# Laying softmax reciprocals by block, and moving logit sums and row evictions between engines, in an attention and expert kernel

## The chip, the cores and the metric

The kernel runs on one core of a Trainium2 chip. The metric is the device time of one execution in microseconds (us). A core has TensorE (matrix products; PE in the profile, and PEld for its weight loads), VectorE (DVE), ScalarE (ACT), GpSimd (POOL) and SyncE (SP, which issues DMAs). Each engine runs its own instructions in the order in which the program gives them, and waits for the others on semaphores.

## The reference, cut to what matters

```
scores = q @ k^T / sqrt(64)                  # q, k, v: 8 batches, 8 heads, 576 rows, 64 columns
attn = exp(scores - max), zero where scores < max - tau
attn = attn / (sum(attn) + 1e-9)
x = (attn @ v) as 4608 rows of 512           # row = batch and position, 8 heads side by side
logits = x @ w_gate                          # 8 experts
each row gets one expert: (row, expert) pairs by falling logit, at most 576 rows for an expert
out[rows of e] = relu(x[rows of e] @ w1[e]) @ w2[e]
```

All is in float32.

## The kernel before, in words

There are two stages: attention (`attention`, the first 469 us of the span) and the experts (`Router`, `moe`). The change is in the first.

**Tiles and slots.** A batch has four pairs of heads. For each pair the 576 rows of both heads make nine tiles of 128 rows: tiles 0 to 7 hold 128 rows of one head each, tile 8 holds the last 64 rows of both heads, head 0 on partitions 0 to 63 and head 1 on 64 to 127. That last block is called the tail here. The loop over `s_` goes in slots of two tiles and is a software pipeline written out by hand: in slot `s_` TensorE computes the scores of tiles `2s+4` and `2s+5` (`score`, L69, into the PSUM tile `sc`, two buffers), VectorE scales them and takes the row maximum (`mx`, L74), GpSimd adds tau to get the threshold `nb` (L75), ScalarE takes the exponential (`ex`, L86), VectorE zeroes what lies under the threshold and sums the row into `den` (`stt`, L90) for the two tiles before, TensorE transposes the two tiles before those (`tr`, L98, into the one buffer `tb`), and ScalarE evicts what was transposed in the slot before (`trev`, L113 and L115). Transposes of the tail go through `left`, and ScalarE evicts them in `leftev` (L125 to L128).

**Product with v.** It is queued in `queue` with a slot for each piece and taken out by `columns`, after the scores of the slot. Columns 0 to 255 of a batch's 576 accumulate in the PSUM bank `xo0`, columns 256 to 575 in `xo1` (`pv_unit`, L152; `pl_unit`, L162 for the tail keys). ScalarE evicts each into `xt` (`evict`, L142). Within a slot L162, or a first piece of L152, can open `xo1` directly behind the scores.

**What a batch leaves.** After the last pair of batch b, `rd_calc` makes the reciprocals `rd` of `den` on VectorE, and `finish(b)` appends units to `aux`. `whole` takes one of them out at the end of a slot when bank `xo1` is free; TensorE fills the bank, the returned function goes to `later`, and `flush` runs it in the next slot, behind the scores and ahead of `trev`. The units are:
- `lg_unit` (two): products of `xt` with the gate weights, four heads' pairs at 32-partition offsets (L179), evicted by ScalarE (L184). The first also multiplies the tail's reciprocals by the constant matrix `swap` (L181), which exchanges the partition halves, and four VectorE copies of 64 partitions (L186, L187) put both heads' reciprocals on both halves, in `rm`.
- `lgt_unit`: transposes of the logits of blocks 0 to 3 (L191). VectorE multiplies them by the reciprocals in two instructions, one for each head of the pairs (L196), and sums over the eight heads (L197) into `Lg`.
- `lgm_unit`: the same for the tail (L201, L206, L207), on partitions 0 to 63 for even batches and 64 to 127 for odd ones.
- `xt_unit` (five, only for batches 0 and 1 here): transposes of `xt` into rows (L213). VectorE evicts the rows into `xr` (L221), GpSimd copies the eight reciprocals of each row beside them, and a DMA writes both to `xrows`. For the other batches these units run after the attention and ScalarE evicts them (L223).

For the last batch the logit units run straight through, in the two `sc` buffers (`bank_g`), and the router begins behind them. It reads `Lg` for batches 0 to 6 first (`prep(0,28)`), then the rest.

Of the kernel before, what the change touches and what calls it, by code (L numbers as in the profile page):

```python
# [9 lines left out]
F32 = mybir.dt.float32  # L10
# [3 lines left out]
AF = mybir.ActivationFunctionType  # L14
ALU = mybir.AluOpType
AX = mybir.AxisListType
# [3 lines left out]
PPB=8; LTB=1; VTB=4; HOLD=1; XW=520; NBO=2; NDEF=4; XTB=4; XTY=1.05; XT0=2.0; XRB=2  # L20


def attention(ctx, tc, qk, vl, tau, wgd, xrows, xts, Lg, nb_batches, ident, swap, R, after_first):
    nc=tc.nc
    V=nc.vector; A=nc.scalar; G=nc.gpsimd; T=nc.tensor
    NP=nb_batches*4; NT=NP*9
# [28 lines left out]
    SC={}; NBI={}; TH={}; PB={}; DEN={}  # L55
    def den_of(p):
        b=p//4
        if b not in DEN: DEN[b]=wk.tile([128,4,9],F32,name="den")
        return DEN[b]
    def score(t):  # L60

# [8 lines left out]
    ZB={}  # L70
# [16 lines left out]
    def stt(t):  # L87
        p,i=divmod(t,9)
        pv=pview(t)
        V.scalar_tensor_tensor(pv,ZB.pop(t).rearrange("p a b -> p (a b)"),NBI[t][:,1:2],pv,op0=ALU.is_le,op1=ALU.mult,accum_out=den_of(p)[:,p%4,i:i+1])  # L90

# [70 lines left out]
    def bank_g(b,sh):  # L164
        if b<nb_batches-1: return bank_v(sh,1)
        t=ps_s.tile([128,2,512],F32,name="sc")[:,0]
        return t.rearrange("p (a b) -> p a b",a=sh[1]) if len(sh)==3 else t

    RD={}
    def rd_calc(b):  # L170
        rd=wk.tile([128,4,9],F32,name="rd",bufs=XTB+NBO); RD[b]=rd
        V.tensor_scalar(rd,DEN[b],1e-9,None,op0=ALU.add)
        V.reciprocal(rd,rd)
    LT={}
    def lg_unit(b,f):
        if f==0: LT[b]=wk.tile([128,S+D],F32,name="lt",bufs=LTB)
        ps=bank_g(b,[128,512]); q=FQ[f]; n=q.stop-q.start; rd=RD[b]
        for j in range(4):
            T.matmul(ps[32*j:32*j+32,:n],wg[:,j],XT[b][:,j,q],start=True,stop=True,tile_position=(0,32*j))  # L179
        if f==0:  # L180
            T.matmul(ps[:,256:260],swap,rd[:,:,8],start=True,stop=True)  # L181
            rm=wk.tile([128,4,2],F32,name="rm",bufs=XTB+NBO); RD["m",b]=rm
        def ev():
            A.activation(LT[b][:,q],ps[:,:n],AF.Copy)  # L184
            if f==1: G.tensor_scalar(LT[b][:,S:],LT[b][:,S-D:S],1.0,0.0,op0=ALU.mult,op1=ALU.add); return
            V.tensor_copy(rm[0:64,:,0],rd[0:64,:,8]); V.tensor_copy(rm[64:128,:,1],rd[64:128,:,8])  # L186
            V.tensor_copy(rm[0:64,:,1],ps[0:64,256:260]); V.tensor_copy(rm[64:128,:,0],ps[64:128,256:260])  # L187
        return ev
    def lgt_unit(b):
        ps=bank_g(b,[128,4,128])  # L190
        for c in range(4): T.transpose(ps[:,c],LT[b][:,c*128:(c+1)*128],ident)  # L191
        def ev():
            w=wk.tile([128,4,2,4,8],F32,name="lw",bufs=1)
            lv=ps.rearrange("p c (j r) -> p c j r",j=4)
            for h in range(2):
                V.tensor_tensor(w[:,:,h],lv[:,:,:,8*h:8*h+8],RD[b][:,:,h:8:2].rearrange("p j c -> p c j").unsqueeze(3).to_broadcast([128,4,4,8]),op=ALU.mult)  # L196
            V.tensor_reduce(Lg[:,4*b:4*b+4,:],w.rearrange("p c h j e -> p c e (h j)"),axis=AX.X,op=ALU.add)  # L197
        return ev
    def lgm_unit(b):
        ps=bank_g(b,[128,4,128])  # L200
        T.transpose(ps[:,0],LT[b][:,512:640],ident)  # L201
        r=slice(64*(b%2),64*(b%2)+64)
        def ev():
            w=wk.tile([128,4,2,8],F32,name="lwm",bufs=1)
            lv=ps[:,0].rearrange("p (j r) -> p j r",j=4)[:,:,:16].rearrange("p j (h e) -> p j h e",h=2)
            V.tensor_tensor(w[r],lv[r],RD["m",b][r].unsqueeze(3).to_broadcast([64,4,2,8]),op=ALU.mult)  # L206
            V.tensor_reduce(Lg[r,32+b//2,:],w[r].rearrange("p j h e -> p e (j h)"),axis=AX.X,op=ALU.add)  # L207
        return ev
    def xt_unit(b,c,k=1):
        ps=bank_v([128,4,128],k)  # L210
        n=128 if c<4 else 64
        for j in range(4):
            T.transpose(ps[:n,j],XT[b][:,j,c*128:c*128+n],ident)  # L213
        early=b<nb_batches-NDEF-NBO
        if early: xr=wk.tile([128,XW],F32,name="xr",bufs=XRB)
        else: xr=wk.tile([128,2,S],F32,name="pp",bufs=PPB)[:,0,:XW]
        def ev():
            src=RD[b][:,:,2*c:2*c+2] if c<4 else RD["m",b][0:64]
            fv=xr[:n,512:XW].rearrange("p (j h) -> p j h",j=4); xv=xr[:n,:512].rearrange("p (j d) -> p j d",j=4)
            if early:  # L220
                V.tensor_copy(xv,ps[:n]); G.tensor_scalar(fv,src,1.0,0.0,op0=ALU.mult,op1=ALU.add)  # L221
            else:
                A.activation(xv,ps[:n],AF.Copy); A.activation(fv,src,AF.Copy)  # L223
            nc.sync.dma_start(xrows[b*S+c*128:b*S+c*128+n,:],xr[:n])
        return ev

# [1 line left out]

    queue=[]; aux=[]; later=[]; late=[]; late2=[]; st={"last":-9,"slot":0}
    def push_pair(p):
        b,j=divmod(p,4)
        def when(n): return lambda: have.get((p,n),1<<30)+HOLD<=st["slot"]
# [20 lines left out]
    def finish(b):  # L255
        aux.extend([(0,lambda: lg_unit(b,0)),(0,lambda: lg_unit(b,1)),(1,lambda: lgt_unit(b)),(0,lambda: lgm_unit(b))])
        rows=[lambda k=1,c=c: xt_unit(b,c,k) for c in range(5)]
        if nb_batches-NDEF-NBO<=b<nb_batches-NDEF:
            nc.sync.dma_start(xts[b],XT[b]); late2.extend(rows)
        elif b<nb_batches-NDEF: aux.extend([(0,x) for x in rows])  # L260
        else: late.extend(rows)
    def flush():
        for k,g in later: g(); k[0]=True
        later.clear()
    def columns(all=False):
        n=0
        while queue and queue[0][1]():
# [7 lines left out]
        return n  # L275
    def whole():
        if aux and free_v(1) and st["slot"]>=st["last"]+aux[0][0] :
            r=aux.pop(0)[1](); st["last"]=st["slot"]
            later.append((banks[1][-1],r))

    idle=cst.tile([128,128],BF16,name="idle"); V.memset(idle,0.0)
    load(0)
# [7 lines left out]
    for s_ in range(-2,NT//2+2):  # L290
        st["slot"]=s_
        sc_=[t for t in (2*s_+4,2*s_+5) if 0<=t<NT]; tr_=[t for t in (2*s_,2*s_+1) if 0<=t<NT]
        ev_=[t for t in (2*s_-2,2*s_-1) if 0<=t<NT]; tt_=[t for t in (2*s_+2,2*s_+3) if 0<=t<NT]
        p8=[(t//9,n) for n,x in enumerate((tr_,ev_)) for t in x if t%9==8]
        if sc_ and sc_[0]%9==8: sc_.reverse()
        for t in sc_: score(t)
        for p,n in p8: left(p,n,sc_[-1] if sc_ else None)

        flush()
        for t in ev_:  # L300
            p,i=divmod(t,9)
# [623 lines left out]
def build(tc, qk, vl, tau, wgd, cst_d, w1, w2, out, off, nb=8):  # L925
    nc=tc.nc
    with ExitStack() as ctx:
        ctx.enter_context(tc.manual_schedule())
        cp=ctx.enter_context(tc.tile_pool(name="cst",bufs=1))
        dr=ctx.enter_context(tc.tile_pool(name="dr",bufs=1,space=bass.MemoryType.DRAM))  # L930
        xrows=dr.tile([8*S,XW],F32,name="xrows")
        xts=dr.tile([8,128,4,S],F32,name="xts")
        ident=cp.tile([128,128],F32,name="ident"); make_identity(nc,ident)
        swap=cp.tile([128,128],F32,name="swap")
        nc.vector.tensor_copy(swap[:,0:64],ident[:,64:128]); nc.vector.tensor_copy(swap[:,64:128],ident[:,0:64])
        Lg=cp.tile([128,NC_,8],F32,name="Lg")
# [24 lines left out]
```

## Time and profile before

| | |
|---|---|
| median of 3 runs | 990.44 us (988.67 to 991.09) |
| the profiled execution | 993.25 us, of which the span 991.4 us |
| TensorE busy, whole span | 955.4 us (96%) |
| VectorE busy | 782.1 us (79%) |
| ScalarE busy | 635.1 us (64%) |
| GpSimd busy | 261.0 us (26%) |
| granted TensorE clock | 0.988 of full speed |

A row of instructions reads: line, engine, operation, what it writes and reads, shapes, count; behind the bars the busy time and the mean of one in ns, and the idle time in front of them with what ended it. A row of the timeline reads: start, duration, engine, line, operation, count, and in brackets the idle time in front. A row of the waits reads: who waited for whom, the sum in us, how often, the longest. A float32 matrix product shows as two records of the same instruction.

### The profile page before, as it was taken

To read this page: it belongs to the slowest core of one execution; us is meant where nothing else is said; L and a number is where in the kernel's file an instruction comes from. 1 tells how busy PE (TensorE), PEld (TensorE's weight loads), DVE (VectorE), ACT (ScalarE), POOL (GpSimd) and SP (SyncE) were. 2 spreads that over 40 slices of the span, in tenths; PEclk is the share of its full clock that TensorE was granted. 3 is DMA by queue.
4 is the path that set the end of the run, shared out by engine and by line. 5 is a ranking of instruction groups with operands and counts; after the bars stand their busy time and mean duration, and the time that the engine had idled before them with its cause. 6 is when DMAs were issued, how large, how long until landed. Compare 5 with 4: busy or idle time off the path is not lost.

```text
span 991.4 us, 24055 instructions
## 1 busy us (share of the span) xinstructions
PE 955.4 (96%) x9141; PEld 709.3 (72%) x9141; DVE 782.1 (79%) x2158; ACT 635.1 (64%) x1257; POOL 261.0 (26%) x411
## 2 busy tenths in 40 slices
PE   7999999999999999998779999999999999999996
PEld 4556665666566556665679688897988979898995
DVE  7999999999999999995679778687787786525220
ACT  6899989898998999996645344243452534545340
POOL 2333334333333333331020323221302213320202
PEclk9999999999999999999979999999999999999998
DMA  6233244234533233303760605343433435341101
GB/s 252 73 110 121 72 153 151 85 142 148 180 109 121 98 120 93 114 3 139 257 211 20 226 28 172 101 137 110 137 124 118 140 100 166 112 137 47 38 11 42
DMA packets 35858, 116.98 MB, mean 118 GB/s; under 512 B 4384, under 2 KB 5024, under 8 KB 35232
## 3 DMA queue, kind: packets, MB, share of 16 engines
q1 hardware_dynamic: 28352, 92.85, 27.5%
q0 software_dynamic: 5888, 19.03, 6.1%
q10 hardware_dynamic: 1504, 3.59, 1.2%
q8 instruction: 72, 1.18, 0.5%
q14 instruction: 42, 0.34, 0.1%
HBM read 93.01 MB, written 21.38 MB: 115 GB/s over the span
## 4 chain that ended last, share of the span: by engine, by line
PE 83%; DVE 8%; issue 3%; DMA 3%; ACT 2%; POOLq 0%; SPq 0%; DVEq 0%; ACTq 0%
PE pf L791 21%; PE pf L823 19%; PE sc L69 13%; PE xo L152 12%; PE tb L98 8%; DVE pp L90 2%; DVE z L74 2%; PE pt L736 2%; PE xo L162 2%; PE xo L213 1%; PE rps L444 1%; PE xo L179 1%; DMA out_dram<-y,idx 1%; PE sc L98 1%; DVE cmp L376 1%
## 5 line engine op out<-in xcount | busy, mean ns | idle before, releaser
L75 POOL TENSOR_SCALAR nb<-nb,taub 128x1 f32<-128x1 f32 x288 | 149.7, 520 | 286.6 <-DVE z L74 246.4
L86 ACT ACTIVATE pp<-z,nb 128x576 f32<-128x576 f32 x256 | 193.5, 773 | 44.3 <-DVE z L74 40.2
L74 DVE TENSOR_SCALAR_CACHE_REDUCE z<-sc 128x576 f32<-128x576 f32 x288 | 205.8, 750 | 10.7 <-PE sc L69 8.8
L90 DVE SCALAR_TENSOR_TENSOR pp<-z,nb,pp 128x576 f32<-128x576 f32 x256 | 199.8, 813 | 0.3
L823 PE MATMUL pf<-w2h,H 128*128 128x512 f32 x576 | 195.2, 402 | 0.7 <-DVE H L376 0.7
L69 PE MATMUL sc<-qk 64*128 64x288 f32 (+1 forms) x1280 | 181.3, 427 | 3.2 <-DVE z L74 1.3
L152 PE MATMUL xo<-pt,vt 128*64 128x320 f32 (+1 forms) x1024 | 156.3, 422 | 0.0
L113 ACT ACTIVATE pt<-tb 128x512 f32<-128x512 f32 x256 | 139.4, 590 | 2.5 <-PE tb L98 1.6
L823 PE MATMUL pf<-w2l,H 128*128 128x512 f32 x320 | 128.3, 401 | 0.0
L830 POOL DMA_INDIRECT out_dram<-y,idx x40 | 43.8, 1096 | 310.3 <-ACT y L826 242.1
L823 PEld LDWEIGHTS pf<-w2h,H 128*128 128x128 f32 x576 | 106.5, 189 | 20.2 <-DVE H L376 1.6
L98 PEld LDWEIGHTS tb<-ident,pp 64*128 64x128 f32 x2048 | 75.2, 139 | 60.1 <-issue 25.5
L69 PEld LDWEIGHTS sc<-qk 64*128 64x128 f32 (+1 forms) x1280 | 94.6, 180 | 31.8 <-DVE z L74 5.7
L791 PE MATMUL pf<-xh,w1h 128*128 128x288 f32 (+2 forms) x512 | 110.1, 301 | 0.7 <-ACT xh L737 0.7
L791 PE MATMUL pf<-xl,w1h 128*128 128x288 f32 (+2 forms) x512 | 110.1, 301 | 0.0
L791 PE MATMUL pf<-xh,w1l 128*128 128x288 f32 (+2 forms) x512 | 109.8, 300 | 0.0
L826 ACT ACTIVATE y<-pf 128x512 f32<-128x512 f32 x40 | 23.9, 598 | 129.0 <-PE pf L823 120.8
L152 PEld LDWEIGHTS xo<-pt,vt 128*64 128x64 f32 x1024 | 61.2, 136 | 59.3 <-issue 33.1
L98 PE MATMUL tb<-ident,pp 64*128 64x64 f32 x2048 | 94.0, 229 | 5.8 <-ACT pt L113 5.8
L803 ACT ACTIVATE hf<-pf 128x576 f32<-128x576 f32 x56 | 36.6, 653 | 90.8 <-PE pf L791 81.7
L791 PEld LDWEIGHTS pf<-xh,w1h 128*128 128x128 f32 x512 | 82.0, 190 | 1.5 <-ACT xh L737 1.1
L791 PEld LDWEIGHTS pf<-xh,w1l 128*128 128x128 f32 x512 | 82.0, 189 | 0.5 <-issue 0.4
(199 smaller groups left out, 1322.4 us busy)
## 6 DMA issues: line engine op xcount, KB each, us to landing
qk<-qk_dram SPq DMA_DIRECT2D x31, 864.0 KB, 4.7
vt<-vl_dram SPq DMA_DIRECT2D x32, 576.0 KB, 3.8
w2s<-w_dram SPq DMA_DIRECT2D x32, 512.0 KB, 5.1
w1s<-w_dram SPq DMA_DIRECT2D x28, 512.0 KB, 4.3
xrows<-pp SPq DMA_DIRECT2D x24, 260.0 KB, 2.2
xts<-xt SPq DMA_DIRECT2D x2, 1152.0 KB
pt<-xts SPq DMA_DIRECT2D x2, 1152.0 KB, 8.7
xrows<-xr SPq DMA_DIRECT2D x8, 260.0 KB, 2.2
```

What stands on the lines that cost most here:

```text
L69: T.matmul(sc[o,f,:HS], kd["q",h][r,c], kd["k",h][r,:],start=True,stop=True)
L74: V.tensor_scalar(z,SC.pop(t)[:,:,:HS],-0.125,None,op0=ALU.mult,op1=ALU.min,accum_out=nb[:,0:1])
L75: G.tensor_scalar(nb[:,1:2],nb[:,0:1],taub[:,0:1],None,op0=ALU.add)
L86: A.activation(pview(t),ZB[t].rearrange("p a b -> p (a b)"),AF.Exp,bias=NBI[t][:,0:1],scale=-1.0)
L90: V.scalar_tensor_tensor(pv,ZB.pop(t).rearrange("p a b -> p (a b)"),NBI[t][:,1:2],pv,op0=ALU.is_le,op1=ALU.mult,accum_out=den_of(p)[:,p%4, ...
L98: g=slice(64*r,64*r+64); T.transpose(o[:,r],x[r%len(x)][g],ident[g,g])
L113: A.activation(PT[p][:,i%2,:,(i//2)*128:(i//2+1)*128].rearrange("p k (r q) -> p r k q",r=2),tb,AF.Copy)
L152: T.matmul(xo[64*h:64*h+64,:q.stop-q.start],v[:,f,128*u+64*h:128*u+64*h+64],PT[p][:,h,u,q],start=new,stop=last,skip_group_check=True)
L791: T.matmul(ps[:,h,:n],s[w][:,k,f*128:(f+1)*128],s[x][:,k,cols[h]],start=(i==0),stop=(i==11))
L803: A.activation(hf,ps[:,:,:HS],AF.Relu)
L823: T.matmul(ps[:,0,:],H[:,f,c:c+128],s[w][:,f],start=(f==0 and j==0),stop=e)
L830: G.indirect_dma_start(out=out,out_offset=IOA(ap=s["idx"][:n,t:t+1],axis=0),in_=y[:n],in_offset=None)
```

## The change

- `den` and `rd` are laid by block of 128 rows, `[128, 5, 4, 2]`: block, pair of heads, head. In the tail's block, GpSimd sets all eight columns to one when the tile is made; `stt` writes head 0's column.
- The matrix `swap` and the tile `rm` go. `dup` holds two matrices: the product with `dup[:,h]` puts the tail's reciprocals of head h on both partition halves. Two products (in `twice`) write eight columns behind the logits in the bank, and one ScalarE copy puts them back into `rd`. The four VectorE copies go.
- `logits` serves blocks and tail alike: one VectorE product for both heads, and the sum over heads as three GpSimd additions, halving each time. The last batch keeps VectorE's reduction. `lw` (one buffer) is now shared by both uses.
- ScalarE evicts the rows of batches 0 and 1 as of the others. In these slots the eviction is put into `behind` and runs after the slot's `trev`, not ahead of it.

```diff
-        if b not in DEN: DEN[b]=wk.tile([128,4,9],F32,name="den")
+        if b not in DEN: DEN[b]=wk.tile([128,5,4,2],F32,name="den"); G.memset(DEN[b][:,4],1.0)
...
-accum_out=den_of(p)[:,p%4,i:i+1])
+accum_out=den_of(p)[:,i//2,p%4,i%2:i%2+1])
...
+    def lg_ev(b,f,ps):
+        q=FQ[f]; A.activation(LT[b][:,q],ps[:,:q.stop-q.start],AF.Copy)
+    def twice(b,ps):
+        for h in range(2):
+            T.matmul(ps[:,:,h],dup[:,h],RD[b][:,4,:,0],start=True,stop=True)
+    def lg_unit(b,f):
+        ps=bank_g(b,[128,512]); rd=RD[b]
+        lg_mm(b,f,ps)
+        if f==0: twice(b,ps[:,256:264].rearrange("p (j h) -> p j h",h=2))
         def ev():
-            A.activation(LT[b][:,q],ps[:,:n],AF.Copy)
+            lg_ev(b,f,ps)
             if f==1: G.tensor_scalar(LT[b][:,S:],LT[b][:,S-D:S],1.0,0.0,op0=ALU.mult,op1=ALU.add); return
-            V.tensor_copy(rm[0:64,:,0],rd[0:64,:,8]); V.tensor_copy(rm[64:128,:,1],rd[64:128,:,8])
-            V.tensor_copy(rm[0:64,:,1],ps[0:64,256:260]); V.tensor_copy(rm[64:128,:,0],ps[64:128,256:260])
+            A.activation(rd[:,4].rearrange("p j h -> p (j h)"),ps[:,256:264],AF.Copy)
...
+    def logits(b,c0,c1,ps,r,o):
+        n=c1-c0; w=wk.tile([128,4,4,2,8],F32,name="lw",bufs=1)[r,:n]; m=r.stop-r.start
+        lv=ps[r].rearrange("p c (j r) -> p (c j) r",r=32)[:,:,:16].rearrange("p m (h e) -> p m h e",h=2)
+        V.tensor_tensor(w.rearrange("p c j h e -> p (c j) h e"),lv,RD[b][r,c0:c1].rearrange("p c j h -> p (c j) h").unsqueeze(3).to_broadcast([m,4*n,2,8]),op=ALU.mult)
+        if b==nb_batches-1: V.tensor_reduce(Lg[r,o:o+n,:],w.rearrange("p c j h e -> p c e (j h)"),axis=AX.X,op=ALU.add); return
+        G.tensor_tensor(w[:,:,0:2],w[:,:,0:2],w[:,:,2:4],op=ALU.add); G.tensor_tensor(w[:,:,0],w[:,:,0],w[:,:,1],op=ALU.add)
+        G.tensor_tensor(Lg[r,o:o+n,:],w[:,:,0,0],w[:,:,0,1],op=ALU.add)
...
-            src=RD[b][:,:,2*c:2*c+2] if c<4 else RD["m",b][0:64]
+            src=RD[b][:n,c]
...
-            if early:
-                V.tensor_copy(xv,ps[:n]); G.tensor_scalar(fv,src,1.0,0.0,op0=ALU.mult,op1=ALU.add)
-            else:
-                A.activation(xv,ps[:n],AF.Copy); A.activation(fv,src,AF.Copy)
+            A.activation(xv,ps[:n],AF.Copy)
+            if early: G.tensor_scalar(fv,src,1.0,0.0,op0=ALU.mult,op1=ALU.add)
+            else: A.activation(fv,src,AF.Copy)
...
-        elif b<nb_batches-NDEF: aux.extend([(0,x) for x in rows])
+        elif b<nb_batches-NDEF: aux.extend([(0,x,behind) for x in rows])
...
             trev(t); have[p,f"t{i}"]=s_
+        flush(behind)
...
-        swap=cp.tile([128,128],F32,name="swap")
-        nc.vector.tensor_copy(swap[:,0:64],ident[:,64:128]); nc.vector.tensor_copy(swap[:,64:128],ident[:,0:64])
+        dup=cp.tile([128,2,128],F32,name="dup")
+        for h in range(2):
+            for a in range(2): nc.vector.tensor_copy(dup[:,h,64*a:64*a+64],ident[:,64*h:64*h+64])
```

More of the change, by code (lines that the diff above doesn't have):

```diff
@@ L20, with attention @@
 PPB=8; LTB=1; VTB=4; HOLD=1; XW=520; NBO=2; NDEF=4; XTB=4; XTY=1.05; XT0=2.0; XRB=2
-def attention(ctx, tc, qk, vl, tau, wgd, xrows, xts, Lg, nb_batches, ident, swap, R, after_first):
+def attention(ctx, tc, qk, vl, tau, wgd, xrows, xts, Lg, nb_batches, ident, dup, R, after_first):
     nc=tc.nc
@@ L89, in stt @@
         pv=pview(t)
-        V.scalar_tensor_tensor(pv,ZB.pop(t).rearrange("p a b -> p (a b)"),NBI[t][:,1:2],pv,op0=ALU.is_le,op1=ALU.mult,accum_out=den_of(p)[:,p%4,i:i+1])
+        V.scalar_tensor_tensor(pv,ZB.pop(t).rearrange("p a b -> p (a b)"),NBI[t][:,1:2],pv,op0=ALU.is_le,op1=ALU.mult,accum_out=den_of(p)[:,i//2,p%4,i%2:i%2+1])
     PT={}; PL={}; TB={}
@@ L170, in rd_calc @@
     def rd_calc(b):
-        rd=wk.tile([128,4,9],F32,name="rd",bufs=XTB+NBO); RD[b]=rd
+        rd=wk.tile([128,5,4,2],F32,name="rd",bufs=XTB+NBO); RD[b]=rd
         V.tensor_scalar(rd,DEN[b],1e-9,None,op0=ALU.add)
@@ L174, in attention, with lg_mm @@
     LT={}
-    def lg_unit(b,f):
+    def lg_mm(b,f,ps):
         if f==0: LT[b]=wk.tile([128,S+D],F32,name="lt",bufs=LTB)
-        ps=bank_g(b,[128,512]); q=FQ[f]; n=q.stop-q.start; rd=RD[b]
+        q=FQ[f]; n=q.stop-q.start
         for j in range(4):
             T.matmul(ps[32*j:32*j+32,:n],wg[:,j],XT[b][:,j,q],start=True,stop=True,tile_position=(0,32*j))
-        if f==0:
-            T.matmul(ps[:,256:260],swap,rd[:,:,8],start=True,stop=True)
-            rm=wk.tile([128,4,2],F32,name="rm",bufs=XTB+NBO); RD["m",b]=rm
+    def lg_ev(b,f,ps):
[7 more added lines that the diff above has]
+        if f==0: twice(b,ps[:,256:264].rearrange("p (j h) -> p j h",h=2))
         def ev():
-            A.activation(LT[b][:,q],ps[:,:n],AF.Copy)
+            lg_ev(b,f,ps)
             if f==1: G.tensor_scalar(LT[b][:,S:],LT[b][:,S-D:S],1.0,0.0,op0=ALU.mult,op1=ALU.add); return
-            V.tensor_copy(rm[0:64,:,0],rd[0:64,:,8]); V.tensor_copy(rm[64:128,:,1],rd[64:128,:,8])
-            V.tensor_copy(rm[0:64,:,1],ps[0:64,256:260]); V.tensor_copy(rm[64:128,:,0],ps[64:128,256:260])
-        return ev
+            A.activation(rd[:,4].rearrange("p j h -> p (j h)"),ps[:,256:264],AF.Copy)
+        return ev
+    def logits(b,c0,c1,ps,r,o):
[5 more added lines that the diff above has]
+        G.tensor_tensor(Lg[r,o:o+n,:],w[:,:,0,0],w[:,:,0,1],op=ALU.add)
     def lgt_unit(b):
@@ L191, in lgt_unit @@
         for c in range(4): T.transpose(ps[:,c],LT[b][:,c*128:(c+1)*128],ident)
[L192 to L198, printed above, removed]
+        return lambda: logits(b,0,4,ps,slice(0,128),4*b)
     def lgm_unit(b):
@@ L201, in lgm_unit @@
         T.transpose(ps[:,0],LT[b][:,512:640],ident)
[L202 to L208, printed above, removed]
+        return lambda: logits(b,4,5,ps[:,0:1],slice(64*(b%2),64*(b%2)+64),32+b//2)
     def xt_unit(b,c,k=1):
@@ L217, in ev @@
         def ev():
-            src=RD[b][:,:,2*c:2*c+2] if c<4 else RD["m",b][0:64]
+            src=RD[b][:n,c]
             fv=xr[:n,512:XW].rearrange("p (j h) -> p j h",j=4); xv=xr[:n,:512].rearrange("p (j d) -> p j d",j=4)
-            if early:
-                V.tensor_copy(xv,ps[:n]); G.tensor_scalar(fv,src,1.0,0.0,op0=ALU.mult,op1=ALU.add)
-            else:
-                A.activation(xv,ps[:n],AF.Copy); A.activation(fv,src,AF.Copy)
+            A.activation(xv,ps[:n],AF.Copy)
+            if early: G.tensor_scalar(fv,src,1.0,0.0,op0=ALU.mult,op1=ALU.add)
+            else: A.activation(fv,src,AF.Copy)
             nc.sync.dma_start(xrows[b*S+c*128:b*S+c*128+n,:],xr[:n])
         return ev
-    queue=[]; aux=[]; later=[]; late=[]; late2=[]; st={"last":-9,"slot":0}
+    queue=[]; aux=[]; later=[]; behind=[]; late=[]; late2=[]; st={"last":-9,"slot":0}
     def push_pair(p):
@@ L259, in finish, with flush @@
             nc.sync.dma_start(xts[b],XT[b]); late2.extend(rows)
-        elif b<nb_batches-NDEF: aux.extend([(0,x) for x in rows])
+        elif b<nb_batches-NDEF: aux.extend([(0,x,behind) for x in rows])
         else: late.extend(rows)
-    def flush():
-        for k,g in later: g(); k[0]=True
-        later.clear()
+    def flush(l=later):
+        for k,g in l: g(); k[0]=True
+        l.clear()
     def columns(all=False):
@@ L277, in whole @@
         if aux and free_v(1) and st["slot"]>=st["last"]+aux[0][0] :
-            r=aux.pop(0)[1](); st["last"]=st["slot"]
-            later.append((banks[1][-1],r))
+            x=aux.pop(0); r=x[1](); st["last"]=st["slot"]
+            (x[2] if len(x)>2 else later).append((banks[1][-1],r))
     idle=cst.tile([128,128],BF16,name="idle"); V.memset(idle,0.0)
@@ L940, in build @@
         with ExitStack() as actx:
-            start=attention(actx,tc,qk,vl,tau,wgd,xrows,xts,Lg,nb,ident,swap,R,load_cst)
+            start=attention(actx,tc,qk,vl,tau,wgd,xrows,xts,Lg,nb,ident,dup,R,load_cst)
         pp=ctx.enter_context(tc.tile_pool(name="rp",bufs=1,space=PSUM))
```

## The prediction

> **What bounds the kernel now.** I read the engine totals first, then the span in four stretches, then the waits and the chain inside the long one.
>
> ```profile
> PE 955.4 (96%) x9141; PEld 709.3 (72%) x9141; DVE 782.1 (79%) x2158; ACT 635.1 (64%) x1257; POOL 261.0 (26%) x411
> ```
> ```profile
> core 0: us, PE busy (x) PEld busy (x) DVE busy (x) ACT busy (x) POOL busy (x), PEclk, DMA share, GB/s
> 0.00:41.00 41.00, 33.55 (x358) 20.63 (x358) 34.41 (x112) 28.55 (x49) 12.97 (x32) 1.00 0.53 189
> 41.00:435.00 394.00, 392.84 (x4749) 236.69 (x4747) 386.91 (x1100) 358.70 (x693) 138.73 (x270) 1.00 0.34 115
> 435.00:469.00 34.00, 30.53 (x347) 17.53 (x343) 25.54 (x77) 24.00 (x52) 8.09 (x13) 1.00 0.22 84
> ```
>
> Everything that the diff touches lies in the attention, the first 469 us, and nearly all of it between 41 and 435 us. There TensorE (392.84 of 394) and VectorE (386.91) both look full, and busy shares cannot say which one leads. The waits of that stretch can: the reader should look at how rarely TensorE stood still for anybody.
>
> ```profile
> PE sc L69 <- DVE z L74: 1.1, 1, 1.1
> PE sc L69 <- ACT pl L128: 0.8, 2, 0.7
> PE xo L162 <- DVE xr L221: 0.3, 1, 0.3
> ```
> ```profile
> by line: PE sc L69 31.3%; PE xo L152 29.8%; PE tb L98 18.8%; PE xo L162 3.9%; issue 2.4%; DVE pp L90 2.4%; PE xo L179 2.2%; DVE z L74 2.0%; PE sc L98 1.9%; PE xo L213 1.3%; PE xo L191 0.7%; ACT pp L86 0.6%; PE xo L181 0.6%; DVE pm L90 0.4%;
> ```
>
> TensorE waited 2.2 us in 394, and the chain runs through it for over 90%. VectorE is full but level with it, not ahead of it on the path. So VectorE work that goes away in this stretch buys at most what TensorE waits there, about 2 us; instructions added to TensorE's queue, or a PSUM bank given back later to it, are paid in full.
>
> **The change part by part.** The profiled execution took 993.25 us, of which the span is 991.4; that is 2.8 above the median of the runs, 990.44. I sum changes in the span and add them to the median.
>
> *The `dup` product.* One product with `swap` per batch becomes two with halves of `dup`; each product is two records.
>
> ```profile
> L181 PEld LDWEIGHTS xo<-rd,swap x14: 186/188/189, 80.8 to 416.8; 128*128 128x128 f32 x14
> L181 PE MATMUL xo<-rd,swap x14: 252/263/273, 80.8 to 416.9; 128*128 128x4 f32 x14
> 463.62 0.38 PE L181 MATMUL sc<-rd,swap 128*128 128x4 f32 x2
> ```
>
> Two records of 0.26 fill 0.38, so they start 0.12 apart. Two more cost 0.24 per batch by that, 0.38 if the weight loads (0.188) do not overlap. Seven batches lie on TensorE's path: 7 x 0.24 = **+1.7 us**, at most 2.6. I take the start distance, since the trace shows it.
>
> *The rows of batches 0 and 1.* Ten evictions from bank xo1 move from VectorE to ScalarE, and `behind` puts them after the slot's two `trev` evictions instead of at the slot's start.
>
> ```profile
> L221 DVE COPY xr<-xo 128x512 f32<-128x512 f32 (+1 forms) x10 | 6.8, 682 | 0.0
> L223 ACT ACTIVATE pp<-xo 128x512 f32<-128x512 f32 (+1 forms) x30 | 17.8, 595 | 6.3 <-ACT pp L223 4.7 <-PE xo L213 1.2
> 111.27 0.78 ACT L86 ACTIVATE pp<-z,nb 128x576 f32<-128x576 f32 x1 [0.40 <-DVE z L74]
> 113.26 1.06 ACT L113 ACTIVATE pt<-tb 128x512 f32<-128x512 f32 x2
> 113.89 0.92 PE L162 MATMUL xo<-pl,vt 64*64 64x256 f32 x8
> 125.50 1.08 ACT L113 ACTIVATE pt<-tb 128x512 f32<-128x512 f32 x2
> 126.36 1.19 PE L152 MATMUL xo<-pt,vt 128*64 128x256 f32 x8
> 139.22 0.78 ACT L86 ACTIVATE pp<-z,nb 128x576 f32<-128x576 f32 x1 [0.51 <-DVE z L74]
> 141.21 1.06 ACT L113 ACTIVATE pt<-tb 128x512 f32<-128x512 f32 x2
> 141.98 0.78 PE L162 MATMUL xo<-pl,vt 64*64 64x256 f32 x8
> ```
>
> The bank's next user is the thing to look for. In four of the ten slots it is the second half of L162, in four the 320-column half of L152, in two the next row's transposes, late enough to wait for nothing. Take 141: the two `trev` occupy ScalarE until 142.2, the row then needs 0.60, and the L162 products that now start at about 142.0 start at 142.9: +0.9. Take 125: `trev` until 126.5, row until 127.1, and the L152 products that start 0.48 into the group, at 126.84, start at 127.15: +0.3. Take 113: +0.8 by the same working, of which I give 0.3 back, because ScalarE idled 0.40 for VectorE just before and VectorE will be earlier. So: +0.5 (113), +0.9 (141), +0.3 (198, where ScalarE idles before too and TensorE waits for the row already: the 0.3 in the waits above), +0.9 (226, like 141: the slot before holds a row too), four times +0.3: **+3.8 us**. Ends: 0, if ScalarE comes early enough everywhere; 6.2, if nothing is given back (4 x 0.9, 4 x 0.35, and 0.6 at each of the other two). In the slot before 141 the extra 0.60 falls into the 0.51 that ScalarE idles, so nothing is queued behind it to speak of. The transposes wait for `trev` of the slot before them, which is not moved.
>
> *Reciprocals and logits on VectorE.* Gone are the `rm` copies and seven of the eight reductions of each kind; two products of 128 elements become one of 256.
>
> ```profile
> L186 DVE COPY rm<-rd 64x4 f32<-64x4 f32 x16 | 2.6, 161 | 0.1
> L187 DVE COPY rm<-xo 64x4 f32<-64x4 f32 x14 | 2.2, 160 | 0.4 <-ACT lt L184 0.2
> L197 DVE TENSOR_REDUCE Lg<-lw 128x32 f32<-128x256 f32 x8 | 5.0, 620 | 0.3
> L207 DVE TENSOR_REDUCE Lg<-lwm 64x8 f32<-64x64 f32 x8 | 2.1, 264 | 0.3
> ```
>
> With the rows' 6.8 that is 6.8 + 2.6 + 2.2 + 4.3 + 1.8 = 17.7 us off VectorE, all of it beside TensorE's work. What it buys is waits of TensorE. One place has rows: the L162 group at 310.53, held by the logits of a tail on VectorE, against an undisturbed one.
>
> ```profile
> 310.53 1.17 PE L162 MATMUL xo<-pl,vt 64*64 64x256 f32 x8
> 449.23 0.71 PE L162 MATMUL xo<-pl,vt 64*64 64x256 f32 x8
> ```
>
> 1.17 - 0.71 = **-0.5 us**; ends 0 and -2.2, all of TensorE's waits. The eight-column copy that replaces the `rm` copies on ScalarE takes 0.2 per batch (ScalarE is busy 358.70 of 394) and frees the bank no later than VectorE did.
>
> *The sums on GpSimd.* Three additions per unit, two units in each of seven batches.
>
> ```profile
> POOL nb L75 <- DVE z L74: 207.8, 170, 2.5
> L185 POOL TENSOR_SCALAR lt<-lt 128x64 f32<-128x64 f32 x8 | 2.0, 245 | 18.4 <-ACT lt L184 18.4
> L833 POOL TENSOR_TENSOR y<-y,z 64x512 f32<-64x512 f32 x2 | 2.6, 1290 | 0.1
> 301.92 0.28 POOL L75 TENSOR_SCALAR nb<-nb,taub 128x1 f32<-128x1 f32 x1 [1.45 <-DVE z L74]
> 302.60 0.71 POOL L75 TENSOR_SCALAR nb<-nb,taub 128x1 f32<-128x1 f32 x1 [0.40 <-DVE z L74]
> ```
>
> Between 0.245 (64 elements) and 1.29 (512), I estimate 0.3 to 0.5 each, 1.3 us per unit. The thresholds `nb` queue behind them; a threshold is wanted a slot (2.8 us) after its maximum, and GpSimd idles 207.8 us waiting for VectorE, so I cost them at **nothing**. Without that cover each unit costs its 0.5 to 1 us of VectorE wait, up to 7 us for seven batches. A threshold takes 0.28 alone and 0.71 beside L90, which reads z and pp. [...]
>
> *End of the attention.* Here the chain leaves TensorE.
>
> ```profile
> 444.59 1.48 DVE pp L90 x4
> 446.23 0.26 DVE Lg L207
> 446.78 0.31 issue
> 447.20 0.78 ACT pp L86
> 464.10 0.38 ACT L184 ACTIVATE lt<-sc 128x256 f32<-128x256 f32 x1 [0.76 <-PE sc L181]
> 464.77 0.44 ACT L184 ACTIVATE lt<-sc 128x320 f32<-128x320 f32 x1 [0.29 <-PE sc L179]
> 465.74 0.49 DVE L196 TENSOR_TENSOR lw<-sc,rd 128x128 f32<-128x128 f32 x2 [0.87 <-PE sc L191]
> ```
>
> The reduction at 446.23 is on the chain and goes to GpSimd: **-0.3 us** (0 to -1). In batch 7 the second `dup` product delays both L184 evictions by 0.24 and one product of some 0.42 replaces 0.49: **+0.2 us** (-0.1 to 0.4). The two extra `dup` copies at the start lie beside the first loads; the `memset` of ones lies in GpSimd's idle time. The expert stage after 469 us does the same work.
>
> Sum: 1.7 + 3.8 - 0.5 - 0.3 + 0.2 = +4.9; 990.44 + 4.9 = **995.3 us**.
>
> **The rivals.**
> *VectorE is the bound* (faster). What decides is whether TensorE keeps its own pace or is handed work by VectorE. For it: 386.91 of 394, and the chain's 5% in L90 and L74. Against it: TensorE's 2.2 us of waits. If all 17.7 us counted: 990.4 - 17.7 + 1.7 = 974.4. [...]
> *ScalarE is early enough* (same). VectorE's relief pulls the exponentials forward, ScalarE reaches the rows 0.4 to 0.9 sooner, and the 3.8 shrinks to 0.8: 1.7 + 0.8 - 0.9 - 0.3 + 0.2 = +1.5, 991.9 us. For it: the idles of 0.40 and 0.51. Against it: at 141 and 125 `trev` follows work that ScalarE itself is behind with, or transposes that TensorE has just ended.
> *GpSimd collides* (slower still): the additions run beside L90, thresholds come late, VectorE and then TensorE stand: +4.9 + 7 = 1002.3. For it: 0.71 against 0.28. Against it: the 207.8 us of idle, and that two L74, which read PSUM, come right behind the product.
>
> **How the numbers follow.** This kernel's measurement cannot tell changes under about 0.3%, 3 us. Forecast 0.59, early ScalarE 0.27, VectorE bound 0.07, GpSimd 0.07. Low end: 1.7 + 0 - 2.2 - 1 - 0.1 = -1.6, 988.8; high end without a GpSimd collision: 2.6 + 6.2 + 0.4 = 9.2, 999.6. I give 989 to 1000, which leaves out most of the first and last rival. Faster 0.08 (the VectorE rival and a little beyond the low end), same 0.29 (the early ScalarE and the forecast's own lower end), slower 0.63.
>
> **What would show it.** Right: TensorE still fills the stretch after 41 us; VectorE's busy time there falls by some 17 us and its waits for `sc` (L69) grow; L162 and L152 wait for the rows' eviction on ScalarE in eight slots between 113 and 240 us; four L181-like records per batch. Wrong: attention ends clearly before 468 us (VectorE led), L162 waits for no row (early ScalarE), or L90 waits for `nb` (GpSimd).

## The result, and the profile after

The changed kernel took 992.32 us (median; 989.85 to 994.96), the kernel before, on the same chip, 988.61 us (986.58 to 991.71). The ratio is 1.0035 with an interval of [1.0025, 1.0046]: 3.5 us slower by the ratio, 3.7 between the medians. The forecast was 4.9 slower, with a range of 1.4 faster to 9.6 slower. The profiled execution after has a span of 993.2 us (before 991.4).

The engine totals, and the same stretches as before the change (columns: us, then the busy time of each engine with its instructions, the granted clock, DMA share, GB/s):

```profile
PE 959.8 (97%) x9157; PEld 712.7 (72%) x9157; DVE 768.5 (77%) x2096; ACT 642.4 (65%) x1275; POOL 265.7 (27%) x461
```
```profile
core 0: us, PE busy (x) PEld busy (x) DVE busy (x) ACT busy (x) POOL busy (x), PEclk, DMA share, GB/s
0.00:41.00 41.00, 33.32 (x356) 20.57 (x358) 34.36 (x114) 28.30 (x49) 12.89 (x33) 1.00 0.53 189
41.00:435.00 394.00, 392.41 (x4718) 235.62 (x4718) 370.60 (x1033) 362.28 (x702) 143.62 (x312) 1.00 0.34 115
435.00:469.00 34.00, 31.54 (x369) 17.95 (x365) 25.23 (x70) 25.33 (x54) 8.64 (x20) 1.00 0.19 71
```

VectorE is busy 386.91 - 370.60 = 16.3 us less in the long stretch, and the kernel became slower. Not all of that is work that went: the kernel after runs up to 4 us late there, so a part of its work falls behind 435 us. Over the whole span VectorE's busy time fell from 782.1 to 768.5 us, by 13.6, and this is the figure used below. TensorE is as full as it was. What grew is VectorE's own idle time and TensorE's waits for the rows. These are waits between 41 and 435 us of the kernel after (who for whom: us, times, longest):

```profile
engine line waited for: us in total, times, longest us
POOL nb L75 <- DVE z L74: 197.8, 163, 2.6
DVE z L74 <- PE sc L69: 19.7, 30, 1.1
POOL lw L199 <- DVE lw L197: 11.6, 12, 1.0
PEld xo L162 <- ACT xr L220: 2.3, 4, 0.7
PEld xo L152 <- ACT xr L220: 2.3, 4, 0.6
PE xo L162 <- ACT xr L220: 0.3, 1, 0.3
```

The same row of before, in the same stretch:

```profile
DVE z L74 <- PE sc L69: 3.6, 8, 1.1
```

The time that VectorE saved it spends waiting for scores. TensorE's weight loads wait in eight places for the eviction that moved to ScalarE. Weight loads overlap products (235.62 us of loads beside 392.41 of products in these 394), so their 4.6 us are an upper bound of what TensorE lost there; the next paragraph counts it on TensorE itself.

**Slot by slot.** The scores of a slot (L69) always stand in the same order on TensorE, so I took the start of each slot's scores in the two traces and subtracted. The difference moves in steps (times are those of the kernel before):

| after minus before | us |
|---|---|
| up to the second slot | +0.24 |
| seven steps of 0.22 at the batches' first logits (81.7 to 417.6) | +1.56 |
| eight row slots: 116, 128, 144, 156, 201, 213, 229, 241 us | +0.49 +0.34 +0.64 +0.32 -0.09 +0.35 +0.71 +0.32 = +3.08 |
| waits that went: 313, 396, 408 us | -0.46 -0.23 -0.17 = -0.86 |
| the difference at 417.6 us (sum, but for rounding) | +4.04 |
| first logits of the last batch (L179), at 462.6 us before and 466.3 after | +3.64 |
| first product of the router behind them (L444), at 469.5 and 473.3 us | +3.87 |

So the whole loss lies in the attention: the end of the last batch gives 0.4 back, and its logits take 0.23 of that again. The expert stage differs between executions of one kernel by more than this (17.1 and 13.3 us at half the clock in the two profiles of the kernel after, as shown at the end).

### The profile page after: what moved, and what is told of

Its sections match the earlier page's. It is cut to its first block, busy times and chain, and to the rows that moved or that the text cites. A ratio compares the mean times of both kernels' runs of the same rounds, so it can differ in the third digit from the quotient of the medians.

```text
span 993.2 us, 24145 instructions
## 1 busy us (share of the span) xinstructions
PE 959.8 (97%) x9157; PEld 712.7 (72%) x9157; DVE 768.5 (77%) x2096; ACT 642.4 (65%) x1275; POOL 265.7 (27%) x461
## 4 chain that ended last, share of the span: by engine, by line
PE 80%; ACT 7%; DVE 7%; issue 3%; DMA 2%; POOLq 0%; DVEq 0%; ACTq 0%; POOL 0%
PE pf L791 22%; PE pf L823 19%; PE sc L69 11%; PE xo L152 11%; PE tb L98 7%; ACT pp L86 3%; PE pt L736 2%; ACT pt L113 2%; PE xo L162 2%; DVE pp L90 1%; DVE z L74 1%; PE xo L213 1%; PE rps L444 1%; PE xo L179 1%; DMA out_dram<-y,idx 1%
## 5 line engine op out<-in xcount | busy, mean ns | idle before, releaser
L74 DVE TENSOR_SCALAR_CACHE_REDUCE z<-sc 128x576 f32<-128x576 f32 x288 | 206.2, 752 | 28.5 <-PE sc L69 25.0
L75 POOL TENSOR_SCALAR nb<-nb,taub 128x1 f32<-128x1 f32 x288 | 142.9, 496 | 267.1 <-DVE z L74 227.7
L90 DVE SCALAR_TENSOR_TENSOR pp<-z,nb,pp 128x576 f32<-128x576 f32 x256 | 199.9, 813 | 0.1
L69 PE MATMUL sc<-qk 64*128 64x288 f32 (+1 forms) x1280 | 181.0, 427 | 3.1 <-DVE z L74 2.2
L69 PEld LDWEIGHTS sc<-qk 64*128 64x128 f32 (+1 forms) x1280 | 94.7, 180 | 31.2 <-DVE z L74 5.7
```

Of the source, the lines that this page charges most:

```text
L69: T.matmul(sc[o,f,:HS], kd["q",h][r,c], kd["k",h][r,:],start=True,stop=True)
L74: V.tensor_scalar(z,SC.pop(t)[:,:,:HS],-0.125,None,op0=ALU.mult,op1=ALU.min,accum_out=nb[:,0:1])
L75: G.tensor_scalar(nb[:,1:2],nb[:,0:1],taub[:,0:1],None,op0=ALU.add)
```

## The experiments

All ratios are against the kernel before, run beside it on the same chip. In the diffs `-` is the kernel after and `+` the experiment, unless said otherwise. "Net of the start" means by the slots, up to the last of them, without what two traces differ by up to 46 us: that is the first row above, and in some executions a difference in the first slots and in the granted clock (last section).

**Does VectorE lead? Its relief undone with idle work.** VectorE gets about the work back that it lost, writing into a tile that nobody reads.

```diff
+    def fill(n): V.tensor_reduce(junk[:,0:n//100],ident[:,0:100]....to_broadcast([128,n//100,100]),axis=AX.X,op=ALU.add)
...
+            for i in range(4): V.tensor_copy(junk[...],ident[...])   # behind L192
+        fill(500 if n==4 else 100)                                    # ahead of the GpSimd sums
+            if early: fill(500)                                       # beside each row
```

> The changed kernel, with VectorE given back as much work as the change took from it, at the same places (a reduction of 500 or 100 elements beside each GpSimd sum, four 64-partition copies for each batch, a reduction of 500 beside each early row), whose results nobody reads. TensorE leads: only TensorE's own waits for VectorE come back, the 0.9 us that left at 310, 393 and 405 us and part of the 0.4 at the end of the attention, so 0.5 to 1.5 us over the changed kernel, +4 to +5.5 us over the kernel before. VectorE leads between 41 and 435 us: all of the refilled 18 us counts, +20 us or more over the kernel before.

Measured: 1.0049 [1.0029, 1.0069], +4.9 us. The window from 41 to 435 us of this run:

```profile
41.00:435.00 394.00, 391.72 (x4708) 235.15 (x4706) 381.84 (x1081) 360.01 (x700) 147.68 (x311) 1.00 0.33 115
```

In this window VectorE is busy 11.2 us more than in the kernel after. Over the whole span it is 781.8 us, so 13.3 of the 13.6 are back:

```profile
PE 960.4 (96%) x9157; PEld 712.1 (72%) x9157; DVE 781.8 (79%) x2152; ACT 641.4 (64%) x1275; POOL 274.2 (28%) x461
```

The kernel is about 1 us slower for it, within the intervals of the two. By the slots +5.14 against +3.80 net of the start: the row slot at 201 us costs 0.55, and the later waits come back in part. VectorE does not lead; its relief was worth some 1.3 us, all of it waits of TensorE.

**Does TensorE lead? Two more tiny products in a batch.**

```diff
-        for h in range(2):
+        for h in (0,1,0,1):
```

> The changed kernel with the two products with dup computed twice, so four for each batch. TensorE leads: two more products are four more records, 0.22 us as the second product of the change costs at its two records 0.11 apart, so 0.45 us for each of eight batches, 3.6 us over the changed kernel, +7.3 us over the kernel before. VectorE leads, or the rows and sums alone explain the loss: TensorE has room and the time stays that of the changed kernel, +3.7.

Measured: 1.0076 [1.0050, 1.0102], +7.5 us, 3.4 to 4.0 above the two timings of the kernel after. The products in the kernel after (four records) and here (eight records), on the timeline (start, duration, engine, line):

```profile
81.07 0.61 PE L184 MATMUL xo<-rd,dup 128*128 128x4 f32 x4
```
```profile
78.09 1.05 PE L184 MATMUL xo<-rd,dup 128*128 128x4 f32 x8
```

Four records more lengthen the group by 0.44. By the slots each batch step is 0.67 against the kernel before, where that of the kernel after is 0.22, so it grew by 0.45: the lengthening of the group and nothing beside it. Eight batches make 3.6, as expected, and the ratios show 3.4 to 4.0, with an interval for this run that is 5 us wide. An engine that does 0.45 us more in each of eight batches costs more than one that does 13 us more in all: that is what leading means.

**The rows' place: evicted by ScalarE ahead of `trev`.**

```diff
-        elif b<nb_batches-NDEF: aux.extend([(0,x,behind) for x in rows])
+        elif b<nb_batches-NDEF: aux.extend([(0,x) for x in rows])
```

> The changed kernel with ScalarE's row evictions of batches 0 and 1 at the start of the slot, ahead of the two transposes' evictions, where VectorE's were. Place decides: the eight waits for bank xo1 (0.3 to 0.7 us each, 3.1 us against the kernel before) go, and the evictions of the transposes come 0.6 later, which the 0.9 us between them and the next transposes hides: 2.5 to 3 us under the changed kernel, +0.5 to +1.2 over the kernel before. ScalarE's load decides, wherever the row stands: transposes then wait instead, and it stays at +3 to +4. GpSimd's sums decide: no change, +3.7.

Measured: 0.9959 [0.9941, 0.9976], 4.1 us *faster* than before (2.6 between the medians), which I had not expected. I timed it again with the kernel after beside it:

> The changed kernel with the rows on ScalarE at the start of the slot, once more. By slots, 4.4 us under the changed kernel and 0.6 under the kernel before, with the end of the attention -1; its first timing said -2.5 to -4.1. Theory: -0.5 to -1.5. If the first timing was right: -2.5 or less, and something that the slots do not show is gained as well.

> The changed kernel once more, beside the mended ones on one chip: +3 to +4.5 us over the kernel before.

Measured: 0.9988 [0.9976, 1.0001], -1.2 us, and for the kernel after 1.0041 [1.0022, 1.0060], +4.1 us. The first -4.1 did not come again, and the granted clock of its executions accounts for a part of it (last section); what holds is 5.6 us between the two medians of this chip (986.77 and 992.33) for one word in the program. The slots give 4.4 of it, and the intervals allow both: all eight row steps are gone, and the kernel before's own waits at 116, 144 and 201 us with them (-0.21, -0.07, -1.04). The slot at 141 us, in the kernel after and with the rows ahead:

```profile
142.38 1.06 ACT L113 ACTIVATE pt<-tb 128x512 f32<-128x512 f32 x2
143.31 1.42 PE L162 MATMUL xo<-pl,vt 64*64 64x256 f32 x8
143.34 0.58 ACT L220 ACTIVATE xr<-xo 128x512 f32<-128x512 f32 x1
143.97 0.19 PEld L162 LDWEIGHTS xo<-pl,vt 64*64 64x64 f32 x4 [0.51 <-ACT xr L220]
```
```profile
138.53 0.58 ACT L220 ACTIVATE xr<-xo 128x512 f32<-128x512 f32 x1
139.00 1.06 ACT L113 ACTIVATE pt<-tb 128x512 f32<-128x512 f32 x2
139.52 0.71 PE L162 MATMUL xo<-pl,vt 64*64 64x256 f32 x8
```

In the first, the eight records of L162 take 1.42, because the second four wait until the row has left the bank behind two `trev`. In the second the row is out at 139.11 and the same eight records take 0.71. The window of the whole stretch with the rows ahead shows TensorE almost without a gap. ScalarE is busier in it than in the kernel after, since more of the work fits into the window:

```profile
41.00:435.00 394.00, 393.96 (x4800) 238.87 (x4802) 375.86 (x1048) 366.38 (x711) 146.61 (x319) 1.00 0.33 115
```

**The rows' engine: VectorE again, still ahead of `trev`.** The edit above, and

```diff
-            A.activation(xv,ps[:n],AF.Copy)
+            V.tensor_copy(xv,ps[:n]) if early else A.activation(xv,ps[:n],AF.Copy)
```

> The changed kernel with the rows of batches 0 and 1 evicted by VectorE at the start of the slot, as before; blocks, dup and GpSimd's sums stay. Theory: of the 3.7 us the rows' 3.1 go, and TensorE's waits for VectorE's rows come back in part (1.3 us in the kernel before, less with VectorE relieved of reductions and copies): +0 to +1.2 over the kernel before. Rival, GpSimd's sums or the layout make the loss: +3 to +4.

Measured: 0.9989 [0.9968, 1.0010], -1.1 us, beside rows_ahead's first timing of -4.1; their medians were 990.61 and 989.95. I had expected +0 to +1.2. By the slots VectorE's rows cost 0.4 more (-0.26 against -0.62 net of the start: small waits at 140 and 196 us). The engine matters little; the place in its queue cost what the kernel after lost.

**The rows alone, in the kernel before.** Here `-` is the kernel before; `behind` is added as in the change.

```diff
-                V.tensor_copy(xv,ps[:n]); G.tensor_scalar(fv,src,1.0,0.0,...)
+                A.activation(xv,ps[:n],AF.Copy); G.tensor_scalar(fv,src,1.0,0.0,...)
...
+        flush(behind)
```

> The kernel before with one part of the change alone: ScalarE evicts the rows of batches 0 and 1, behind the slot's two evictions of transposes. Theory: the eight later hand-overs of bank xo1 cost what they cost in the changed kernel, 3.1 us net, and nothing of the 0.9 us at 310 to 405 us comes off: +2.5 to +3.5 us over the kernel before. Rival, the loss is in dup, the sums or the layout: -1 to +1.

Measured: 1.0041 [1.0024, 1.0058], +4.1 us by the ratio, +2.7 between medians. By the slots: no batch steps, the row steps .79 .34 .65 .32 .67 .34 .71 .32 (4.1), and the waits at 313, 396 and 408 us stay. Against the kernel after, two row steps are larger (0.79 for 0.49, 0.67 for -0.09): there the rest of the change had relieved VectorE, and ScalarE came earlier.

**One product in place of two.** The reciprocals go into two masked columns for each pair, and one matrix doubles both partition halves.

```diff
+        V.tensor_tensor(rm,rd[:,4,:,0:1].to_broadcast([128,4,2]),dup[1],op=ALU.mult)
...
-        for h in range(2):
-            T.matmul(ps[:,:,h],dup[:,h],RD[b][:,4,:,0],start=True,stop=True)
+        T.matmul(ps,dup[0],RD["m",b],start=True,stop=True)
```

The two constants are made on GpSimd at the start.

> The changed kernel with one product in place of two: VectorE multiplies the tail's reciprocals by a mask of the two halves (128x8, once for each batch), and one product with the sum of both dup matrices writes all eight columns; the constants are made on GpSimd. TensorE leads: two records of 0.11 less for each of eight batches and 0.2 less at the start, 2.0 us under the changed kernel, +1.5 to +2 over the kernel before; VectorE's added 0.2 for each batch costs nothing. Rival, TensorE's small products are hidden: +3.7, or more by VectorE's work.

Measured: 1.0009 [0.9993, 1.0024], +0.9 us. The batch steps are gone, and by the slots the kernel stands at +2.36 net of the start (+3.80 after). With the start (0.2) and the logits of the last batch (0.2), which that figure leaves out, its trace stands 1.9 under that of the kernel after, where I had expected 2.0. By timing it gains more, 2.6 to 3.2; the intervals allow both, and at equal clock the difference goes (last section).

**The sums back on VectorE.**

```diff
-        if b==nb_batches-1: V.tensor_reduce(Lg[r,o:o+n,:],...); return
+        if True: V.tensor_reduce(Lg[r,o:o+n,:],...); return
```

> The changed kernel with the sums over heads left to VectorE for all batches, as for the last; GpSimd adds nothing. Theory: GpSimd's sums buy only TensorE's waits for VectorE's reductions, 0.5 to 1 us, so +4 to +5 over the kernel before. Rival 1, VectorE's 6.2 us count: +9 to +10. Rival 2, GpSimd's additions collide with VectorE: they go, +1 to +3.

Measured: 1.0052 [1.0030, 1.0073], +5.2 us: not faster than the kernel after, so the additions on GpSimd have no cost that shows. By the slots the VectorE reductions cost 1.7 (+5.49 net of the start): most of the -0.86 is lost (only 0.07 of it is left), and two row steps grow.

**Both repairs together, and the router's constants spread.** The first kernel has the rows ahead and the one product. The second also takes `R.consts` apart: at 37 us VectorE makes the router's constants in one block, and here one of eleven pieces is put behind each of pairs 1 to 13.

```diff
-        if (b,j)==(0,0): queue.append(("n",lambda: True,False,R.consts,p))
+        if p==0: R.some=R.consts()
+        if 0<p<14: queue.append(("n",lambda: True,False,lambda: next(R.some,None),p))
```

> The changed kernel with both mends: ScalarE's rows at the start of the slot, and one product in place of two. By slots rows ahead gave 4.4 us of the changed kernel back, one product should give 2.0: 2 to 3 us under the kernel before, so -2 to -4.5 with what the runs of rows_ahead measured (-2.5 between medians, -4.1 by ratio). If the two mends overlap: as rows_ahead.

> Rows at the start of the slot and one product, once more: 2.0 us under rows_ahead on the same chip, by eight times 0.22 and the start.

> Rows at the start of the slot, one product, and the router's constants, some 20 small VectorE instructions that stand in one block of 2.4 us at 37 us, are spread in eleven pieces over the pairs 1 to 13. Theory: before 41 us VectorE leads and the block is paid in full, behind 41 us TensorE leads and VectorE has the room that the change made, so 2.4 us come off, and TensorE's pause at 40 us with it, after which it ran at half clock for 3.4 us in some executions: 2 to 4 us under best_again. Rival, VectorE leads behind 41 us as well: no gain, the same work elsewhere.

Measured: both repairs 0.9971 [0.9951, 0.9991] (-2.9 us), and again, on the chip of rows_ahead's second timing, 0.9986 [0.9973, 1.0000] (-1.4). There it should have stood 2.0 under rows_ahead and stood 0.6 above it (987.33 and 986.77). By the slots it is 1.4 ahead, net of the start. Why the time did not follow stays open in part; what the granted clock accounts for is told at the end.

With the constants spread: 983.04 us, 0.9954 [0.9938, 0.9970], -4.5 us, 4.3 under both repairs on the same chip. It is faster than the kernel before and the kernel after. The block stood where VectorE led and TensorE waited. Before, on the timeline:

```profile
38.65 0.72 PE L98 MATMUL tb<-ident,pp 64*128 64x64 f32 x16
40.49 0.76 PE L69 MATMUL sc<-qk 64*128 64x288 f32 x4 [1.13 <-DVE z L74]
41.94 1.33 PE L69 MATMUL sc<-qk 64*128 64x288 f32 x4 [0.69 <-ACT pl L128]
```

and with the constants spread:

```profile
38.82 0.71 PE L98 MATMUL tb<-ident,pp 64*128 64x64 f32 x16
39.36 1.20 PE L69 MATMUL sc<-qk 64*128 64x288 f32 x8
40.49 1.19 PE L152 MATMUL xo<-pt,vt 128*64 128x256 f32 x8
```

The pauses of 1.13 and 0.69 are gone. VectorE has that work still, in the stretch where it only waits for TensorE: there it is busier than with both repairs alone (377.19 in the profile of their second timing), and TensorE has no gap.

```profile
41.00:435.00 394.00, 394.00 (x4808) 238.45 (x4806) 379.29 (x1077) 366.32 (x713) 147.94 (x322) 1.00 0.34 115
```

## Why the prediction was right, point by point

- **What bounds.** TensorE led; the run with VectorE refilled and the run with four products bear it out from both sides. But the waits of 2.2 us from which the prediction took this, and which it made the bound of what VectorE's relief could buy, are not all of TensorE's waits. That view counts the products' waits only; where the weights of a product wait, the row stands under PEld. The group at 310.53, which the prediction itself priced at 0.5, is not among the 2.2. It stands under PEld, and only with a part of its length; and after the change the view of the products shows 2.1 although the rows alone held TensorE up for 4.4. First the row of PEld before, then TensorE's products after:

```profile
PEld xo L162 <- DVE lwm L206: 0.3, 1, 0.3
```
```profile
PE sc L69 <- DVE z L74: 1.1, 1, 1.1
PE sc L69 <- ACT pl L128: 0.7, 1, 0.7
PE xo L162 <- ACT xr L220: 0.3, 1, 0.3
```

  The first two rows of the products are the pause at 40 us, which the change does not touch. So the conclusion was right and the bound of 2.2 was no bound; that the relief, 13.6 us less on VectorE, bought about 1.3, below it, was luck. (The 17.7 us of the prediction is a sum of single durations; the engine's busy time fell by less.)
- **The `dup` product: +1.7 forecast, +1.56 measured.** The start distance was the right price. The records start 0.11 to 0.13 apart, two more cost 0.22 instead of 0.24, and the weight loads of 0.19 overlap:

```profile
L184 PEld LDWEIGHTS xo<-rd,dup x28: 186/190/192, 81.1 to 420.9; 128*128 128x128 f32 x28
L184 PE MATMUL xo<-rd,dup x28: 252/253/273, 81.1 to 420.9; 128*128 128x4 f32 x28
```

- **The rows: +3.8 forecast, +3.08 net measured.** The eight slots named by the bank's next user were the eight that waited. TensorE's waits on rows were 0.71 0.34 0.71 0.32 0.94 0.35 0.71 0.32 (4.4), and the kernel before had waited there for 1.3 already. The terms mis-sized are the two of 0.9 and the 0.3 at 198. At 141 (0.64 measured) the two `trev` ended 0.29 behind the start of L162 in the trace of before (142.27 and 141.98) and 0.13 behind it after (143.44 and 143.31), so ScalarE came earlier; the run with the rows alone has 0.65 there, so taking the rows off VectorE was enough for it. At 226 (0.71) the prediction carried the 0.9 over from 141; the trace of before gives 0.73 by the same working (`trev` until 226.90, L162 from 226.77). At 198 (-0.09) a wait of 0.94 was there in full before; with the rows alone 0.67 come on top of it, and the rest of VectorE's relief takes them away. At 113 the 0.3 given back for this was about right (+0.49 for +0.5; +0.79 with the rows alone). So "ScalarE is early enough" was a true mechanism with a small price: 3.1 here against 4.1 with the rows alone.
- **Waits that VectorE's relief ends: -0.5 forecast, -0.86 measured.** Beside the group at 310 (-0.46) two more went, at 396 and 408 (-0.23 and -0.17).
- **GpSimd's sums: nothing forecast, nothing measured.** GpSimd kept 197.8 us of waits for VectorE, and for VectorE the view of the waits names nobody but TensorE in the long stretch, so no L90 waited for `nb` to speak of. The additions took 0.31 and 0.23 in the mean, at the low end of the estimate of 0.3 to 0.5 and below it; the means mix sizes, from 0.20 to 0.45 (columns: busy, mean ns, idle in front):

```profile
L199 POOL TENSOR_TENSOR lw<-lw 128x128 f32<-128x128 f32 (+3 forms) x28 | 8.6, 309 | 14.5 <-DVE lw L197 13.4
L200 POOL TENSOR_TENSOR Lg<-lw 128x32 f32<-128x32 f32 (+1 forms) x14 | 3.2, 225 | 1.1
```

No addition was held up: those of one size differ by at most 0.01 us (the largest took 0.452 to 0.457). None of them ran beside L90, where 143 thresholds took 0.71 in the median; the 142 that started beside L74, which the prediction calls alone, took 0.28. So what the third rival rests on did not come about. Its 7 us was the author's estimate and no run shows it: the run with the sums back on VectorE was no faster than the kernel after, so taking the additions away gained nothing.

- **End of the attention: -0.3 + 0.2 forecast, -0.40 + 0.23 measured.** The wait in front of one group of transposes shrank by 0.40. Before and after:

```profile
452.86 0.71 PE L98 MATMUL tb<-ident,pp 64*128 64x64 f32 x16 [1.59 <-ACT pt L113]
```
```profile
456.50 0.71 PE L98 MATMUL tb<-ident,pp 64*128 64x64 f32 x16 [1.19 <-ACT pt L113]
```

  From the first logits of the last batch to the router's first product it is 6.83 us before and 7.06 after; with one product in place of two it is 6.83 again, so the 0.23 is the second product, as forecast. That the 0.40 is the reduction that left VectorE fits the forecast, but no run takes it apart cleanly.
- **The set-up: nothing forecast, +0.2 measured.** Two more copies of `dup` on VectorE stand ahead of the `memset` for which TensorE's first products wait, 2.1 us before and 2.3 after:

```profile
PE xo L288 <- DVE idle L281: 2.1, 1, 2.1
```
```profile
PE xo L287 <- DVE idle L280: 2.3, 1, 2.3
```

"Beside the first loads" was true of the loads, and I had not asked who waits for VectorE there.

The sum of these terms is 0.24 + 1.56 + 3.08 - 0.86 - 0.40 + 0.23 = +3.85, beside 3.5 to 3.7 and, the second time, 4.1 by timing. The forecast of 4.9 was 1.05 above this sum, most of it (0.72) in the rows.

## What to carry to other kernels

Where two engines look full, count the waits of each, TensorE's weight loads with its products. Relief of the one that follows is worth only the leader's waits for it (here 1.3 of 13.6 us), and work can go onto it at little cost. An eviction moved to another engine is priced by its new place in that engine's queue against the next user of the bank: the same ten evictions cost TensorE 4.4 us of waits behind two others of the slot and none ahead of them. And a block of set-up work belongs where its engine follows, in pieces, not where it leads (here 4.3 us between two medians).

## What the runs showed that I had not expected

After TensorE's pause at 40 us, its granted clock falls in some executions and not in others, of the same kernel too: its mean from 41 to 46 us is 0.66 in one profile of the kernel after and 1.00 in the other. The window from 41 to 46 us of the kernels before, after, and with the rows ahead:

```profile
41.00:46.00 5.00, 4.31 (x34) 1.96 (x32) 4.52 (x14) 3.87 (x9) 1.71 (x3) 0.66 0.00 2
```
```profile
41.00:46.00 5.00, 4.31 (x30) 1.75 (x28) 4.76 (x14) 4.07 (x9) 1.85 (x4) 0.66 0.00 2
```
```profile
41.00:46.00 5.00, 4.96 (x54) 2.40 (x56) 5.00 (x15) 4.67 (x9) 1.38 (x4) 1.00 0.12 20
```

Taken by single microseconds the clock of the kernel before is 0.50 from 42 to 45 us, so a mean of 0.66 over 5 us is half the clock for 3.4 us. Of the fourteen profiles, some of which are of the same kernel, five show it (before, after, vector_refilled, one_product and best_again), and the slots put its cost at 1.57 us. That is two fifths of the effect studied here, so one profile of each kernel could not have settled it by its span. Without the pause (the constants spread) the clock stayed at 1.00; that is one execution, and eight with the pause stayed there too.

The start of the expert stage has such stretches too, in varying number: in each of ten profiles the clock there is below full speed (means of 0.77 to 0.86 from 478 to 515 us in six of them, of 0.61 to 0.77 from 500 to 515 in four). By single microseconds it is at 0.50 for 3.4 us from 492.5 and for 10.2 from 502.7 in the kernel before, for 3.4 us from 496.2 and for 13.7 from 506.5 in the kernel after. These are 13.7 and 17.1 us; the second profile of the kernel after has 13.3, by a mean of 0.82 from 478 to 515 us. From 478 to 515 us, rows_ahead's second timing and both repairs' second timing:

```profile
478.00:515.00 37.00, 28.53 (x304) 25.02 (x304) 26.53 (x81) 17.81 (x45) 6.23 (x6) 0.86 0.68 230
```
```profile
478.00:515.00 37.00, 28.75 (x286) 25.03 (x285) 25.75 (x74) 16.79 (x43) 6.22 (x6) 0.77 0.69 236
```

0.14 and 0.23 of 37 us below full speed are 10.4 and 17.0 us at half the clock: by estimate, three and five stretches of 3.4. With the stretch at 41 us, which the second of them has as well, this could hide a part of the 2.0 that is missing in that comparison.

The mean granted clock of every execution is on record, not only that of the profiled ones, so times can be compared at equal clock. A straight line laid through all executions of a chip, with a constant for each kernel, gives 0.7 to 1.0 us for 0.001 of the clock. This is an estimate; its differences hold within 0.6 to 1.2 us.

| against the kernel before, us | slots, net of the start | ratio | at equal clock |
|---|---|---|---|
| rows ahead, first timing | -0.6 | -4.1 | -1.6 |
| rows ahead, second timing | -0.6 | -1.2 | -0.6 |
| rows on VectorE, ahead | -0.3 | -1.1 | -0.6 |
| one product | +2.4 | +0.9 | +2.4 |
| both repairs, first timing | -2.1 | -2.9 | -1.9 |
| both repairs, second timing | -2.1 | -1.4 | -1.1 |

For the kernel after (second timing), VectorE refilled, four products, rows only and the sums on VectorE, the slots and the times at equal clock lie within half a microsecond of each other. So the clock explains most of what the timings had beyond the slots in the first rows ahead and in the one product. It does not explain all of the comparison of the two second timings: at equal clock both repairs stand 0.6 ahead of the rows ahead, with an interval from 0.2 behind to 1.3 ahead, where the slots say 1.4.

What sets the stretches off no run shows. In the kernel before, the one at 41 us followed two pauses of 1.13 and 0.69 us; the rows ahead had pauses of 1.14 and 0.69 there and a clock of 1.00 behind them.
